# Three sets' scores masked by ScalarE and GpSimd, and two more parts of the first product by seven multiplications

## The chip, the cores and the metric

The kernel runs on one core of a Trainium2 chip. The metric is the device time in microseconds of one execution; the time of a kernel is the median of its runs. Engines are called by their names or by the profile's: PE (TensorE; PEld is its weight load), DVE (VectorE), ACT (ScalarE), POOL (GpSimd), SP (SyncE, which here only issues DMAs).

## The reference

Linear attention with decay for 4 batches, 8 heads, 768 positions and 64 dimensions, in blocks of 64, followed by a feed-forward layer on its output (3072 tokens of 512 features, 2048 hidden):

```
for b in range(nb):
    intra = einsum('bhic,bhjc->bhij', qb, kb) * Dmask      # Dmask: lam ** (i - j) where i >= j, else 0
    intra = einsum('bhij,bhjd->bhid', intra, vb)
    inter = einsum('bhid,bhde->bhie', qb * lam_pow, kv_state)
    out[:, :, sl] = intra + inter
    kv_state = lam_block * kv_state + einsum('bhsd,bhse->bhde', kb * rev_pow, vb)
h = x @ w_in                      # x: out as [3072, 512]
out = (h / (1 + exp(-h))) @ w_out
```

Inputs and output are float32; the kernel multiplies in bfloat16 and sums in float32.

## The kernel before, in words

The 3072 tokens are 24 units of 128 positions (6 position blocks of 4 batches). The attention takes two units at a time, a **set**: sets 0 to 3 hold blocks 0 and 1 of one batch each, sets 4 to 11 hold one block (2 to 5) of two batches. The feed-forward layer takes four units at a time, a **group** of 512 tokens; groups 2 to 5 are position blocks 2 to 5. In each set q, k and v are loaded by SP (L422), cast and scaled by powers of lam (L718 to L739; the powers are arranged so that the mask within a block becomes a plain triangle of ones and zeros), and q and k are turned, from set 6 on by a DMA transpose (L777). Then TensorE computes scores and state updates (`first_part`, L783), the scores are masked into the tile `st` (`after_first`, L869: two instructions on DVE that multiply the PSUM tile by the triangle `tri`), the states are carried on (`yf`, `y`, `xf`, `xe`), and TensorE computes the outputs (`second_part`, L819) into `x_ps`, which is copied as `xt` (L928), the input of the feed-forward layer. From set 7 on, the second part of one set and the first part of the next are one burst on TensorE.

The first product (x times w_in, then silu into the tiles `g`) has two forms. `product1` (L969) is the plain one: per tile of 128 hidden features four matmuls of 512 columns (L989). `product1_spared` (L1073) is the other: it splits the matrices into 2 x 2 blocks and needs seven block products where the plain form needs eight (`product`, L1106: four matmuls of 256 columns each), with sums of blocks of w_in (`wsum`, made once by DVE, L1053) and of xt (`xsum`, four DVE instructions for each group, L1089), and with copies (`keep`, L1118), totals (`h`, L1131) and four silus for each part. A group's first product has four parts. Before the change, parts 0, 1 and 2 of group 4 and all of group 5 are made by seven. The second product (`product2`, L1197, `products_of`, L1241) is made by seven for all units but the first four; its sums on the left side are the tiles `s`, and its results go through `osb` to the output.

No instruction is placed by hand. Every piece of work is a task with a key, engines that may take it with a cost on each, tasks that it depends on, and buffers from pools of fixed size. A planner (L39 to L215) runs through a timetable of its own before anything is issued: on each engine, whenever it is free, it takes the ready task with the smallest key whose buffers are to be had; a task that names several engines goes to the one that would be done first. The order found in this way is the program's order on every engine, and on the chip each engine works through its own queue in that order. Keys are built from a unit's rank (0 to 23) and from constants: LEAD and HURRY (how far ahead of its rank a set from 4 on is prepared, `key_of`, L521), EAGER and CALM (the same for the small work of the second product), ONTO (from which unit on the first sum of the second product stays in PSUM, L1297), HOLD (how many `two` buffers the first four units by seven hold, L1245), SUMS_ON (the key of the wsum). Pools `one` and `sp` limit how many tiles of the plain and the split first product are open at once. The wsum tiles live in the pool `rb`, which also holds the raw loads of q, k and v.

The mask, as it stands before:

```
def mask(e, p):
    tt(e, o.st_of()[:, p].rearrange("p b m i -> p (b m) i"), o.st_ps[p].tile.rearrange("p b m i -> p (b m) i"),
       tri[:, None, :].to_broadcast([128, nb * NP, 64]), AL.mult)

o.masked = [add((s - 0.9, 0), {"DVE": 0.15 + w / 950}, lambda e, p=p: mask(e, p), deps=[t], bufs=[o.st_ps[p], o.st])
            for p in range(2)]
```

Of the kernel before, what the change touches and what calls it, by code (L numbers as in the profile page):

```python
# [11 lines left out]
AL = mybir.AluOpType  # L12
# [26 lines left out]
class Planner:  # L39
# [16 lines left out]
    def add(self, key, on, fn, deps=(), bufs=(), nbytes=0, kind=None, prior=(), late=0.0):  # L56
        key = key if isinstance(key, tuple) else (key,)
        on = on if nbytes else {e: d - self.OVERLAP.get(e, 0.0) for e, d in on.items()}
        t = Task(key, on, fn, deps, list(bufs) + [b.with_ for b in bufs if b.with_], nbytes, kind, prior, late)
        for b in t.bufs:  # L60
            b.left += 1
        self.tasks.append(t)
        return t
# [155 lines left out]
def kernel(  # L219
# [10 lines left out]
    nc = tc.nc  # L230
# [5 lines left out]
    NP = H // 2  # L236
# [7 lines left out]
    PAIRED = 2  # L244
    SETS = [[(0, b), (1, b)] for b in range(B)] + [[(n, b), (n, b + 1)] for n in range(PAIRED, NB) for b in (0, 2)]
    GROUPS = [SETS[0] + SETS[1], SETS[2] + SETS[3]] + [[(n, b) for b in range(B)] for n in range(PAIRED, NB)]
    FRESH, TURNED, ALONE, LEAD = 4, 6, 6, 4.25
    SEQUENCE = "s0 s1 i0a@1.1 i0b i1a i1b i2a i2b i3a i3b o0 o1 s2@1.0 o2 o3 s3 s4"
    POOLS = dict(bank=8, ra=3, rb=6, kq=3, kqT=3, vd=3, st=3, xe=6, xf=3, y=2, yf=2,
                 xt2=2, xt4=2, g=18, s=12, m=3, osb=3, one=3, two=8, att=6, sp=3)  # L250
    BY_POOL, PLAIN = (), 4
    CASTING, SUMS_AFTER, HURRY, SUMS_ON, HOLD, ONTO = 12, 16, 0.0, 9.0, 1, 24
    EARLY, PACE = 1.0, 1.0
    OPEN, FILLED, SCALED = 4, True, (1,)
    QUERIES = (0, 1, 2, 3)
# [1 line left out]
    ON_ACT = ()  # L257
    LAZY, FINE, SAFE, EASY, TAIL, SURE = 2.0, True, 1.3, -0.22, 0.9, 1.5
    XE_2, XE_B, XE_P = {"ACT": 0.42, "DVE": 0.35}, 0.1, False
    MIXED, APART, KEPT = (0, 1, 2), 1, 'yf'  # L260
    EAGER, CALM, ON = 10.0, 1.0, 0.0
    SHARED = ()
    BY_SET = {0: 8, 1: 16}
    WHOLE = ()
    RATED = (3, 4)
    S3_IN = "rb"

    ctx.enter_context(tc.manual_schedule())
    const = ctx.enter_context(tc.tile_pool(name="const", bufs=1))
# [4 lines left out]
    add = plan.add  # L274

    def tile_of(b, shape, dt, name):
# [9 lines left out]
        out=lam_sb[0:1],  # L286
        in_=bass.AP(tensor=lam.tensor, offset=lam.offset, ap=[[0, 1]] + list(lam.ap)),
# [7 lines left out]
    halves = [slice(0, 64), slice(64, 128)]  # L295
# [12 lines left out]
    for t in xe_tiles[4:]:  # L308
# [6 lines left out]
        out=ident, in_=ident, compare_op=AL.not_equal, fill=1.0,  # L315
        base=0, pattern=[[-1, 128]], channel_multiplier=1,
# [6 lines left out]
    for c, r in enumerate(halves):  # L323
        nc.gpsimd.affine_select(
            out=tri[r], in_=tri[r], compare_op=AL.is_ge, fill=0.0,
            base=0, pattern=[[1, 64]], channel_multiplier=-1,
# [5 lines left out]
    for r in halves:  # L332
        nc.gpsimd.iota(iota_2[r], pattern=[[0, 1]], base=0, channel_multiplier=2)
        for a in range(2):
            for b in range(2):
                nc.gpsimd.affine_select(
                    out=tri_2[r, a, b], in_=tri_2[r, a, b], compare_op=AL.is_ge, fill=0.0,
                    base=-1 if a > b else 0, pattern=[[1, 64]], channel_multiplier=-1,
# [27 lines left out]
    def copy(e, o, i):  # L366
        if e == "ACT":
            nc.scalar.activation(o, i, AF.Copy)  # L368
        elif e == "DVE":
            nc.vector.tensor_copy(o, i)  # L370
        else:
            nc.gpsimd.tensor_copy(o, i)

    def tt(e, o, a, b, op):
        (nc.vector if e == "DVE" else nc.gpsimd).tensor_tensor(o, a, b, op=op)  # L375
# [26 lines left out]
    raw = {}  # L402
    sp_last = []
# [53 lines left out]
    for m, x in enumerate(SEQUENCE.split() + [f"s{i}" for i in range(len(sets))]):  # L457
        x, _, behind = x.partition("@")
        j, part = int(x[1:].rstrip("ab")), x[-1] if x[-1] in "ab" else ""
# [11 lines left out]
        elif behind and behind[0] in "io":  # L471

            ts, wt = wload[behind[0], int(behind[1])], w_in_bf if behind[0] == "i" else w_out_bf
            at = wt[0:1, 0, 512 * int(behind[1]):512 * int(behind[1]) + 1] if behind[0] == "i" else wt[0:1, 4 * int(behind[1]), 0:1]
            held = [add((m - 100, -1), {"SP": 2.2}, lambda e, g=gates, at=at: nc.sync.dma_start(
                out=gate_w[0:1, g:g + 1], in_=at), deps=ts, prior=sp_last[-1:])]
            gates += 1
        elif behind:
            u, i = map(int, behind.split("."))
            rs, loads = raw[u]  # L480
            tile = lambda b=rs[i]: b.tile[:, 0, 0, 0:1] if len(b.tile.shape) == 4 else b.tile[:, 0, 0:1]
            if x[0] == "s":
                held = [add((m - 100, -1), {"SP": 2.2}, lambda e, g=gates, tile=tile: nc.sync.dma_start(
                    out=gate[0:1, g:g + 1], in_=tile()[0:1]), deps=loads[i], bufs=[rs[i]], prior=sp_last[-1:])]
# [12 lines left out]
    groups = GROUPS  # L497
# [7 lines left out]
    def after(stage, ts):  # L505
        ts = ts if isinstance(ts, list) else [ts]
        for t in ts:
            t.deps += chain.get(stage, [])
        chain[stage] = ts
# [9 lines left out]
    infos = []  # L519
# [349 lines left out]
    def after_first(o, t):  # L869

        n, bs, nb, s = o.n, o.bs, o.nb, o.s
        w = 512 * nb // 2

        def mask(e, p):
            tt(e, o.st_of()[:, p].rearrange("p b m i -> p (b m) i"), o.st_ps[p].tile.rearrange("p b m i -> p (b m) i"),
               tri[:, None, :].to_broadcast([128, nb * NP, 64]), AL.mult)

        o.masked = [add((s - 0.9, 0), {"DVE": 0.15 + w / 950}, lambda e, p=p: mask(e, p), deps=[t], bufs=[o.st_ps[p], o.st])
                    for p in range(2)]
        after("m", o.masked)  # L880
        bp = bs[0] // 2
        b0 = bs[0] % 2
        xe_in, xf_in, xe_ready, xf_ready = carry[n - 1, bp]
        o.xe = [xe_in, Buf("xe")]
        dcost = 0.15 + w / 950

        def of(b, dt=F32):
            return tile_of(b, [128, nb, NP, 64], dt, b.pool)

        def blocks(b, src, deps, bufs, i):  # L890

            def go(e, r):
                if b.tile is None:
                    b.tile = xe_tiles[b.slot]
                copy(e, b.tile[halves[r], b0:b0 + nb, :, halves[r]], src()[halves[r]])

            return [add((s - 0.9, i), dict({"ACT": 0.2 + w / 1200, "DVE": XE_B + w / 1900}, **({"POOL": 0.25 + w / 1000} if XE_P else {})), lambda e, r=r: go(e, r),
                        deps=deps, bufs=[b] + bufs) for r in range(2)]

        o.xe_done = list(xe_ready)  # L900
        mf = Buf("yf")
        tm = add((s - 0.9, 1), {"DVE": dcost}, lambda e: tt(e, of(mf), o.d_of(0), xf_in.tile, AL.add),
                 deps=[t] + xf_ready, bufs=[o.d_ps[0], mf, xf_in])
        o.xe_done += blocks(o.xe[1], lambda: mf.tile, [tm], [mf], 2)
        if n == NB - 1:
            return

        y = Buf("y")
        ty = add((s - 0.9, 3), {"DVE": dcost}, lambda e: tt(e, of(y), o.d_of(1), mf.tile, AL.add),
                 deps=[t, tm], bufs=[o.d_ps[1], mf, y])  # L910
        xe_n, xf_n, xe_t, xf_t = carry[n, bp] = Buf("xe"), Buf("xf"), [], []
        rate = lam_be[:, None, :, None].to_broadcast([128, nb, NP, 64])

        def xf_of():
            return tile_of(xf_n, [128, 2, NP, 64], F32, "xf")[:, b0:b0 + nb]

        def next_states(e):
            if e == "DVE":
                tt(e, xf_of(), y.tile, rate, AL.mult)
                return  # L920
            for m in range(NP):
                by_rate(e, xf_of()[:, :, m], y.tile[:, :, m], lam_be[:, m:m + 1])

        tf = add((s - 0.9, 4), {"DVE": dcost, **({"ACT": 1.1} if n in RATED else {})}, next_states, deps=[ty], bufs=[y, xf_n])
        xf_t.append(tf)
        xe_t += blocks(xe_n, xf_of, [tf], [xf_n], 5)
# [21 lines left out]
    for si, o in enumerate(infos):  # L948
# [6 lines left out]
        else:  # L955
            if open_ is None:
                after_first(o, burst((o.s - 0.5, 0), [first_part(o)]))
            else:
                a, b = second_part(open_), first_part(o)
                t = burst((o.s - 0.5, 0), [a, b])  # L960
# [90 lines left out]
            W[f"A{i + 1}{j + 1}"] = lambda r=r, c=c: w_in_bf[:, c, r]  # L1051

    def sums_of_w_in():  # L1053
        bufs = {name: Buf(S3_IN if name == "S3" else "rb") for name in ("S1", "S2", "S3", "S4")}
        for name, b in bufs.items():
            W[name] = lambda b=b: tile_of(b, [128, 2, 1024], BF16, "wsum")
        loads = [t for i in range(4) for t in wload["i", i]]
        done = {"A11": loads, "A12": loads, "A22": loads}
        issued, casts = [sp_last[-1]], [t for ts in infos[-1].ck for t in ts]

        def total(name, a, b, op, deps, on):
            done[name] = [add((on, 8), {"DVE": 0.7}, lambda e, ks=ks: tt(
                e, W[name]()[:, ks], W[a]()[:, ks], W[b]()[:, ks], op), deps=deps, prior=issued, bufs=[bufs[name]])
                          for ks in (0, 1)]

        on = SUMS_ON
        total("S1", "A21", "A22", AL.add, loads, on)
        total("S2", "S1", "A11", AL.subtract, done["S1"], on + 0.1)
        total("S3", "A11", "A21", AL.subtract, casts, on + 0.2)
        total("S4", "A12", "S2", AL.subtract, done["S2"], on + 0.3)  # L1070
        return bufs, done
# [242 lines left out]
        m3 = product(6, R, "S4", "B22", False, [e22])  # L1314
        result(0, hi, R, b2, [m3, c2])

    for gi in range(len(groups) - 2):
        product1(gi)
    for t in waits:
        t.deps += gs[0, 0][2]  # L1320
        t.bufs.append(gs[0, 0][0])
        gs[0, 0][0].left += 1
    made = sums_of_w_in()
    left = [j for j in range(4) if j not in MIXED]
    if left:
        product1(len(groups) - 2, [m for j in left for m in (2 * j, 2 * j + 8)])
    if MIXED:
        product1_spared(len(groups) - 2, *made, MIXED)
    product1_spared(len(groups) - 1, *made, range(4))
    by_rank = sorted(rank, key=rank.get)  # L1330
    for u in by_rank[:PLAIN]:
# [49 lines left out]
```

## Time and profile before

| what | value |
|---|---|
| time, median of 3 runs | 201.17 us (201.0 to 202.44) |
| the profiled execution | 200.99 us, its span 199.2 us |
| matmuls of the first product, plain, 512 columns | 176 |
| matmuls of the first product by seven, 256 columns | 196 |
| masks of scores on DVE, 128x512 from PSUM | 32 |
| POOL in the span | 13.7 us busy, nothing after about 35 us |
| granted TensorE clock | 1.00 |

The profile is of one execution. Its page gives, in this order, the busy time of each engine, the span in 40 slices (a digit is tenths of busy time), the DMA queues, the chain of work that ended last, and the costliest groups of instructions: line, engine, operation, output<-input with shapes, count | busy us, mean ns of one | idle time of the engine ahead of them and what ended it. Other views of the same trace are the chain in order of time, the waits (who waited for whom: us in total, times, longest), and the timeline (start, length, engine and instruction). Lines are those of the kernel before.

### The profile page before, as it was taken

To read this page: it belongs to the slowest core of one execution; us is meant where nothing else is said; L and a number is where in the kernel's file an instruction comes from. 1 tells how busy PE (TensorE), PEld (TensorE's weight loads), DVE (VectorE), ACT (ScalarE), POOL (GpSimd) and SP (SyncE) were. 2 spreads that over 40 slices of the span, in tenths; PEclk is the share of its full clock that TensorE was granted. 3 is DMA by queue.
4 is the path that set the end of the run, shared out by engine and by line. 5 is a ranking of instruction groups with operands and counts; after the bars stand their busy time and mean duration, and the time that the engine had idled before them with its cause. 6 is when DMAs were issued, how large, how long until landed. Compare 5 with 4: busy or idle time off the path is not lost.

```text
span 199.2 us, 5953 instructions
## 1 busy us (share of the span) xinstructions
PE 188.4 (95%) x2564; PEld 139.7 (70%) x2564; DVE 146.1 (73%) x302; ACT 127.4 (64%) x241; POOL 13.7 (7%) x36
## 2 busy tenths in 40 slices
PE   0699799999999999999999999999999999999993
PEld 0467565447778785667778648478888688888882
DVE  7799230278997999939998854999948991986611
ACT  2857767218899947648383785536797847866220
POOL 7087003000000000000000000000000000000000
PEclk9999999999999999999999999999999999999999
DMA  5999999999999999999999999901911001003304
GB/s 155 290 241 194 215 216 217 277 215 236 259 262 233 227 238 199 248 162 211 187 207 221 204 261 195 268 4 59 155 56 56 0 3 53 0 5 105 105 30 133
DMA packets 84894, 32.89 MB, mean 165 GB/s; under 512 B 62852, under 2 KB 84356, under 8 KB 84868
## 3 DMA queue, kind: packets, MB, share of 16 engines
q1 hardware_dynamic: 75074, 22.55, 59.1%
q0 software_dynamic: 4288, 4.20, 12.8%
q10 hardware_dynamic: 5506, 5.77, 9.2%
q8 instruction: 20, 0.33, 0.7%
q14 instruction: 6, 0.05, 0.1%
HBM read 27.26 MB, written 6.29 MB: 168 GB/s over the span
## 4 chain that ended last, share of the span: by engine, by line
PE 87%; DVE 4%; DMA 4%; ACT 1%; SPq 1%; issue 1%
PE o_ps L1259 31%; PE h_ps L989 29%; PE h_ps L1112 11%; PE o_ps L1029 7%; DMA raw<-in_q_dram 4%; DVE st L375 2%; PE x_ps L842 2%; PE d_ps L802 1%; PE x_ps L834 1%; SPq L417 1%; PE st_ps L812 1%; PE tr L768 1%; PE tr L566 1%; ACT xe L368 1%; ACT xt L368 1%
## 5 line engine op out<-in xcount | busy, mean ns | idle before, releaser
L989 PE MATMUL h_ps<-xt,w_in_bf 128*128 128x256 bf16 (+1 forms) x368 | 63.2, 324 | 1.1 <-DVE xt L370 0.6
L989 PEld LDWEIGHTS <-w_in_bf 128*128 128x128 bf16 x368 | 35.0, 98 | 22.4 <-issue 1.3
L1259 PEld LDWEIGHTS <-g 128*128 128x128 bf16 x320 | 31.1, 98 | 4.8
L1006 ACT ACTIVATE g<-h_ps 128x512 bf16<-128x512 f32 x44 | 25.3, 595 | 8.5 <-PE h_ps L989 8.4
L1259 PEld LDWEIGHTS <-s 128*128 128x128 bf16 x240 | 23.4, 98 | 3.0
L375 DVE TENSOR_TENSOR st<-st_ps,tri 128x512 bf16<-128x512 f32 x32 | 20.5, 684 | 5.0 <-PE st_ps L812 5.0
L375 DVE TENSOR_TENSOR vd<-raw,lam_v 128x512 bf16<-128x512 f32 x24 | 15.9, 686 | 7.8 <-DMA raw<-in_v_dram 7.8
L1259 PE MATMUL o_ps<-w_out_bf,s 128*128 128x256 bf16 x160 | 19.1, 273 | 0.0
L1259 PE MATMUL o_ps<-wsum,g 128*128 128x256 bf16 x160 | 18.9, 273 | 0.0
L375 DVE TENSOR_TENSOR kq<-raw,lam_q 128x512 bf16<-128x512 f32 x24 | 15.8, 684 | 4.3 <-DMA raw<-in_q_dram 4.0
L1259 PE MATMUL o_ps<-w_out_bf,g 128*128 128x256 bf16 x160 | 18.6, 273 | 0.0
L1004 ACT ACTIVATE g<-h_ps 128x512 bf16<-128x512 f32 x24 | 13.8, 597 | 6.4 <-PE h_ps L989 6.3
L368 ACT ACTIVATE m<-o_ps 128x512 f32<-128x512 f32 (+1 forms) x16 | 8.5, 528 | 14.4 <-PE o_ps L1259 14.3
L375 DVE TENSOR_TENSOR osb<-o_ps,m 128x512 f32<-128x512 f32 (+1 forms) x18 | 10.8, 599 | 9.2 <-ACT m L368 5.2
L368 ACT ACTIVATE xt<-x_ps 128x512 bf16<-128x512 f32 x16 | 9.8, 640 | 9.1 <-DVE osb L375 3.2
L1029 PE MATMUL o_ps<-w_out_bf,g 128*128 128x512 bf16 x64 | 15.5, 380 | 0.0
L375 DVE TENSOR_TENSOR h<-h_ps,m 128x512 f32<-128x512 f32 x14 | 9.6, 688 | 7.3 <-ACT m L368 7.1
L1112 PEld LDWEIGHTS <-wsum 128*128 128x128 bf16 x112 | 10.9, 98 | 1.5
L368 ACT ACTIVATE kqT<-tr 128x512 bf16<-128x512 bf16 x19 | 10.4, 598 | 2.0 <-PE tr L566 1.5
L368 ACT ACTIVATE kq<-raw 128x512 bf16<-128x512 f32 x16 | 9.7, 627 | 2.2 <-DMA raw<-in_k_dram 2.0
L1112 PE MATMUL h_ps<-xsum,wsum 128*128 128x256 bf16 x84 | 11.0, 273 | 0.0
L1138 ACT ACTIVATE g<-h 128x512 bf16<-128x512 f32 x14 | 8.7, 628 | 2.3 <-DVE h L375 2.2
(98 smaller groups left out, 257.5 us busy)
## 6 DMA issues: line engine op xcount, KB each, us to landing
raw<-in_q_dram SPq DMA_DIRECT2D x12, 512.0 KB, 7.7
raw<-in_k_dram SPq DMA_DIRECT2D x12, 512.0 KB, 7.9
raw<-in_v_dram SPq DMA_DIRECT2D x12, 512.0 KB, 7.4
out_dram<-osb ACTq DMA_DIRECT2D x20, 256.0 KB, 4.4
w_in_bf<-in_moe_w_in_dram POOLq DMA_DIRECT2D x8, 256.0 KB, 8.9
w_out_bf<-in_moe_w_out_dram POOLq DMA_DIRECT2D x4, 512.0 KB, 14.2
out_dram<-osb ACTq DMA_DIRECT2D x4, 128.0 KB, 1.7
out_dram<-osb SPq DMA_DIRECT2D x4, 128.0 KB, 2.0
```

Source lines behind the costliest of these rows:

```text
L368: nc.scalar.activation(o, i, AF.Copy)
L375: (nc.vector if e == "DVE" else nc.gpsimd).tensor_tensor(o, a, b, op=op)
L417: nc.sync.dma_start(out=rs[i].tile.rearrange("p h e d -> p h (e d)"), in_=x[i])
L566: nc.tensor.transpose(t[:, m, a], o.kq_of()[:, i, m, a], ident)
L842: nc.tensor.matmul(x_of(c)[:, j, m, :], lhsT=o.xe[c].tile[:, (bs[0] + j) % 2, m, :], rhs=o.kqT_of()[:, 1, j, m, halves[c]], start=False, s ...
L989: nc.tensor.matmul(t[:, j, :], lhsT=w_in_bf[:, ko, 128 * m:128 * m + 128], rhs=xt[gi].tile[:, ko, ts], start=ko == 0 and (j == 0 or len(ko ...
L1004: nc.scalar.activation(t[:, :, ts], bank.tile, AF.Silu)
L1006: nc.scalar.activation(t[:, x, :], bank.tile[:, 0], AF.Silu)
L1029: nc.tensor.matmul(t, lhsT=g.tile[:, j, 128 * gp:128 * gp + 128], rhs=w_out_bf[:, ko, :], start=(ko == 0), stop=(ko == KO - 1))
L1112: nc.tensor.matmul(t[:, j, :], lhsT=W[w]()[:, k2, f:f + 128], rhs=X(r)[:, k2, :], start=first and j == 0 and k2 == 0, stop=True, skip_grou ...
L1138: nc.scalar.activation(o, src(), AF.Silu)
L1259: nc.tensor.matmul(t[:, i_, :], lhsT=src(j)[:, k2, 128 * r:128 * r + 128], rhs=W[w]()[:, 2 * j + k2, :], start=first and i_ == 0 and j == ...
```

## The change

The mask of sets 6, 8 and 10 is taken from DVE: ScalarE copies the scores from PSUM into `st` (two instructions of 128x512), and GpSimd then clears in place, in each half of the partitions, what lies behind the query (two affine_select instructions of 64 partitions by 1024). Group 4's first product is made by seven in all its four parts, and part 0 of group 3 too. The sums of w_in wait for the load of set 9 and no longer for the last load. Several constants that set keys and pools are changed.

```
-    FRESH, TURNED, ALONE, LEAD = 4, 6, 6, 4.25
+    FRESH, TURNED, ALONE, LEAD = 4, 6, 6, 3.5
-                 xt2=2, xt4=2, g=18, s=12, m=3, osb=3, one=3, two=8, att=6, sp=3)
+                 xt2=2, xt4=2, g=18, s=12, m=3, osb=3, one=4, two=8, att=6, sp=2)
-    CASTING, SUMS_AFTER, HURRY, SUMS_ON, HOLD, ONTO = 12, 16, 0.0, 9.0, 1, 24
+    CASTING, SUMS_AFTER, HURRY, SUMS_ON, HOLD, ONTO = 12, 16, 1.0, 6.0, 0, 20
-    MIXED, APART, KEPT = (0, 1, 2), 1, 'yf'
-    EAGER, CALM, ON = 10.0, 1.0, 0.0
+    MIXED, APART, KEPT = (0, 1, 2, 3), 1, 'yf'
+    EAGER, CALM, ON = 12.0, 2.0, 0.0
+    SUMS_IN, BEHIND = 'rb', 9
+    THIRD = (0,)
+    CUT, CUT_TIME = (6, 8, 10), 1.1
...
-        o.masked = [add((s - 0.9, 0), {"DVE": 0.15 + w / 950}, lambda e, p=p: mask(e, p), deps=[t], bufs=[o.st_ps[p], o.st])
-                    for p in range(2)]
+        if o.si in CUT:
+
+            def taken(e, p):
+                copy(e, o.st_of()[:, p].rearrange("p b m i -> p (b m) i"), o.st_ps[p].tile.rearrange("p b m i -> p (b m) i"))
+
+            def cut(e, r):
+                x = o.st_of()[r].rearrange("p h b m i -> p (h b m) i")
+                nc.gpsimd.affine_select(out=x, in_=x, compare_op=AL.is_ge, fill=0.0, base=0,
+                                        pattern=[[0, 2 * nb * NP], [1, 64]], channel_multiplier=-1)
+
+            tk = [add((s - 0.9, 0), {"ACT": 0.17 + w / 1200}, lambda e, p=p: taken(e, p), deps=[t], bufs=[o.st_ps[p], o.st])
+                  for p in range(2)]
+            o.masked = [add((s - 0.9, 0), {"POOL": CUT_TIME}, lambda e, r=r: cut(e, r), deps=tk, bufs=[o.st]) for r in halves]
+        else:
+            o.masked = [add((s - 0.9, 0), {"DVE": 0.15 + w / 950}, lambda e, p=p: mask(e, p), deps=[t], bufs=[o.st_ps[p], o.st])
+                        for p in range(2)]
...
-        issued, casts = [sp_last[-1]], [t for ts in infos[-1].ck for t in ts]
+        issued, casts = raw[BEHIND][1][2][-1:], [t for ts in infos[BEHIND].ck for t in ts]
...
-    for gi in range(len(groups) - 2):
+    for gi in range(len(groups) - 3):
         product1(gi)
...
+    for gi, parts in ((3, THIRD), (4, MIXED)):
+        left = [j for j in range(4) if j not in parts]
+        if left:
+            product1(gi, [m for j in left for m in (2 * j, 2 * j + 8)])
+        if parts:
+            product1_spared(gi, *made, parts)
     product1_spared(len(groups) - 1, *made, range(4))
```

More of the change, by code (lines that the diff above doesn't have):

```diff
@@ L1053, in sums_of_w_in @@
     def sums_of_w_in():
-        bufs = {name: Buf(S3_IN if name == "S3" else "rb") for name in ("S1", "S2", "S3", "S4")}
+        bufs = {name: Buf(SUMS_IN) for name in ("S1", "S2", "S3", "S4")}
         for name, b in bufs.items():
@@ L1323 @@
     made = sums_of_w_in()
[L1324 to L1328, printed above, removed]
+    for gi, parts in ((3, THIRD), (4, MIXED)):
[4 more added lines that the diff above has]
+            product1_spared(gi, *made, parts)
     product1_spared(len(groups) - 1, *made, range(4))
```

## The prediction

> **What bounds the kernel now.** Read first: busy shares and the chain that ended last, then the chain in order of time, the groups by form, the waits after 76 us, and a piece of the timeline.
>
> ```profile
> PE 188.4 (95%) x2564; PEld 139.7 (70%) x2564; DVE 146.1 (73%) x302; ACT 127.4 (64%) x241; POOL 13.7 (7%) x36
> ...
> PE   0699799999999999999999999999999999999993
> ...
> PEclk9999999999999999999999999999999999999999
> ...
> PE 87%; DVE 4%; DMA 4%; ACT 1%; SPq 1%; issue 1%
> ```
>
> TensorE is busy 95% of the span at full clock and carries 87% of the chain. What is not TensorE lies in the first 22 us and the last three.
>
> ```profile
> 76.58 6.20 PE h_ps L989 x28
> ...
> 98.15 3.45 PE h_ps L989 x16
> ...
> 143.55 4.37 PE h_ps L1112 x40
> ...
> 183.91 12.24 PE o_ps L1259 x112
> 196.16 0.02 issue
> 196.18 0.42 DVE osb L375
> ```
>
> The chain in order of time (start, us, what): from 22.4 to 196.16 us it is TensorE almost without a break. It gives issue intervals: 3.45/16 = 215.6 ns for a matmul of 512 columns, 4.37/40 = 109.3 ns for 256 (12.24/112 says the same). The mean durations below (379 and 273) overlap and cannot be added.
>
> ```profile
> L989 PE MATMUL h_ps<-xt,w_in_bf 128*128 128x512 bf16 x176 | 40.3, 379 | 0.2 <-ACT xe L368 0.2
> ...
> L1006 ACT ACTIVATE g<-h_ps 128x512 bf16<-128x512 f32 x44 | 25.3, 595 | 8.5 <-PE h_ps L989 8.4
> ...
> L375 DVE TENSOR_TENSOR st<-st_ps,tri 128x512 bf16<-128x512 f32 x32 | 20.5, 684 | 5.0 <-PE st_ps L812 5.0
> ...
> L336 POOL TENSOR_SCALAR_AFFINE_SELECT tri<-tri 64x64 f32<-64x64 f32 x8 | 1.6, 241 | 0.1
> ...
> L314 POOL TENSOR_SCALAR_AFFINE_SELECT ident<-ident 128x128 bf16<-128x128 bf16 x1 | 0.3, 287 | 0.1
> ```
>
> ```profile
> PEld L989 <- DVE xt L370: 0.4, 1, 0.4
> ...
> PE h_ps L989 <- ACT xe L368: 0.2, 1, 0.2
> ```
>
> Waits between 76 and 185 us: beyond "issue" the list has only these for TensorE.
>
> ```profile
> 75.38 1.04 PE L989 MATMUL h_ps<-xt,w_in_bf 128*128 128x256 bf16 x8
> ...
> 75.82 0.69 DVE L370 CAST xt<-x_ps 128x512 bf16<-128x512 f32 x1
> ...
> 76.57 3.63 PE L989 MATMUL h_ps<-xt,w_in_bf 128*128 128x512 bf16 x16 [0.15 <-ACT xe L368]
> ```
>
> The one place where TensorE stands: eight matmuls from 75.38 are issued by 75.38 + 8 x 0.109 = 76.25, and block 2's first product starts at 76.57, when set 5's copy of xt (75.82 + 0.69) is done: 0.32 us. So the bound is TensorE's own issue, and no edit to another engine can give more than this.
>
> **The change part by part.** The profiled execution took 200.99 us (span 199.2, 1.79 around it); the median is 201.17. I sum against 200.99. The rest goes by the order in which the changed program's instructions stand on each engine. Up to 73.6 us TensorE's order is the same, and so are the counts of fillers, of second-product matmuls (560 + 64) and of everything else on TensorE but this:
>
> 1. *Two more parts in seven* (block 4's last, block 3's first). 32 matmuls of 512 go, 56 of 256 come: 56 x 0.1093 - 32 x 0.2156 = 6.12 - 6.90 = **-0.78 us**, all on the path.
>
> 2. *The stall at 76.25.* In the new order set 5's second part stands after four matmuls of the split product in place of eight, and twelve follow it in place of eight: 12 x 0.109 = 1.31 us of cover for the copies of xt, where 0.87 was 0.32 short; VectorE's queue before that copy is unchanged in length (a 0.69 osb for a 0.69 kq, a 0.42 s for the other). **-0.32 us**; the bound above is nothing.
>
> 3. *Scores of sets 6, 8, 10.* VectorE loses 6 masks of 684 ns. ScalarE gains 6 copies of 128x512 from PSUM, 0.60 each (row L1006). GpSimd gains 6 clears of 64 partitions x 1024. No row has this shape. A line through the two affine_select rows, 241 ns at 64 elements and 287 at 128, is 0.72 ns per element on a base of 0.195: 0.93 us. Bounds: 0.29 (no growth at all) to 16 x 0.241 = 3.9 (all growth). I take 0.93, since the two rows differ by 46 ns for twice the elements. Path from scores to use: 0.2 + 2 copies (0.60 + 0.50) + 2 clears (1.9) + waits 0.3 = 3.5 us. Cover, summed from the issue intervals in the new order: set 6 from 91.7 to 98.1 = 6.4 us; set 8 from 110.8 to 125.2; set 10 from 132.5 to 155.9. Nothing on the path; it would be for set 6 above (6.4 - 1.6)/2 = 2.4 us a clear.
>
> 4. *What the two parts cost beside TensorE.* Four xsum for block 3 (0.42), four h (0.69) on VectorE, some six copies m (0.60) on ScalarE. Counted over the whole order, VectorE comes to 145 us (4.1 less for masks, 1.7 and 2.8 more, the rest small), ScalarE to 127.4 + 8.1 = 135.5, 68% of the span. In the densest stretch (two parts of block 4 at once, 32 matmuls, 3.5 us) ScalarE must give two silus and two copies between products: at 0.53 apart the last copy is done 3.0 us in, and the product that overwrites its bank starts at 3.06. It holds, with nothing to spare: +0.1.
>
> 5. *Sums of w_in made behind set 9's load.* Eight wsum (0.69) move on VectorE from 138-152 us to about 105-119, and take four of the six raw buffers while sets 10 and 11 are still to load. I find those loads issued in time (transposes of set 10 at about 121, first used at 131.6). The last wsum stands just ahead of the h that the seventh product of block 3's part waits for: VectorE's queue from set 8's yf (111.0) to that h adds up to 7.7 us, h ends at 119.5, the product is due at 120.1: slack 0.1 to 0.5. I put +0.2 there.
>
> 6. *LEAD, HURRY, EAGER, CALM, HOLD, pools one and sp.* They change order alone. On SP the transposes of sets 6 and 7 now stand back to back (about 82 and 86, 3.6 us each by the earlier rows) ahead of the load of set 8's queries, which goes out near 89.8 where it went at 79.75. Loads behind a transpose landed 5.4 and 8.2 us after issue (113.6 to 119.0, 100.4 to 108.6): 95.2 to 98.0. VectorE reaches that query at about 96.2, and queued behind it are the sums that the third product of the next four units needs at 104.6, with some 0.5 us to spare. So 0 to 1.3; I take +0.2. Earlier, the first four units' third product moves from 82.6 to 80.7, and its last sum ends at 80.5: +0.1.
>
> 7. *ONTO 20.* In the last four units the first product's sum is copied into the second's bank. That product now waits for a copy (0.42 on VectorE), but 0.87 us of another product lies between. The end (last matmul, osb 0.42, store) is the same: 0.
>
> Sum: -0.78 - 0.32 + 0.1 + 0.2 + 0.2 + 0.1 = -0.5, so 200.99 - 0.5 = **200.5**. New stalls together are bounded by 0 and about 1.3 + 0.5 + 0.3 without the rivals below.
>
> **The rivals.**
>
> *GpSimd's clears hold VectorE off (slower).* While a clear runs, VectorE's instructions with two operands in SBUF (s, xsum, xf, vd, kq) would stand until it ends. Nothing in this trace shows it either way, as GpSimd computes nothing after 5 us but two one-element copies. Price: up to 0.93 a clear, 1.9 a set. Set 8's clears (about 115 to 117) fall among the vd, xf and wsum that precede the h of point 5: 0.9 (half of them caught) to 1.8 on the path. Set 6's (93 to 95) fall on s and xf before the sums of point 6: 0.4 to 1.3. Set 10's: VectorE is some 2 us ahead, 0. Together 1.3 to 3.1 on 200.5: 201.8 to 203.6, middle **202.6**. It makes the kernel slower than before from 0.5 us of such loss on. The Trainium skill has this as a rule: "SBUF — State Buffer", section "Who interferes with whom", says that a VectorE instruction with two SBUF inputs contends with a GpSimd instruction that reads SBUF, and that whichever comes second is blocked in full until the first is done. By that rule the sum would be this rival's; by the rows alone, 200.5. Against it stands that many of VectorE's neighbours there (yf, y, h, osb) read PSUM, and that ops that come late can be absorbed by slack I counted too low.
>
> *Set 8's load late.* If it lands 8.2 us or more after issue and the transposes take 5.2 (rows at 95 and 108) and not 3.6, VectorE stands 1.8 to 3 us, 1.3 to 2.5 of it on the path: 201.0 to 202.8, middle **201.9**. For it: SP's queue. Against it: fewer loads are in flight then.
>
> *The clear is priced by elements.* At 3.9 us a clear, set 6 is late by 2 x (3.9 - 2.4) = 3.0, and the rest as above: **204**.
>
> *The time falls by more than 1%.* TensorE's order leaves no room: 200.99 - 0.78 - 0.32 = 199.9 with no new stall.
>
> **How the numbers follow.** Forecast 0.58 (own range 199.8 to 201.3), clears hold VectorE 0.22, late load 0.12, dear clear 0.06, beyond the floor 0.02. Range 199.8 to 202.9: it leaves out the last two, and about half of what the clears' case has above 202.6. About 1% is what a measurement of this kernel can tell from no change: 199.2 and 203.2. Faster: 0.02. Slower: the dear clear and a quarter of the clears' case, 0.11. Same: 0.87.
>
> **What would show it.** In the groups, 252 matmuls of the split product and 144 of 512 columns at the same intervals; last matmul near 195.7. No wait at 76. Clears of 0.9 to 1.0 us; VectorE's sums beside them at 0.42 (forecast) or at 1 us and more (rival). Waits of TensorE on "DVE s" near 104.6 or on "DVE h" near 120 add up to about half a microsecond, not two. I am wrong if the interval of the matmuls changes, if the first 73 us differ, or if TensorE stands anywhere for more than 1 us.

## The result: slower by half a per cent, and the profile after

| | before | changed |
|---|---|---|
| time, median (16 runs each) | 201.03 us (200.88 to 202.44) | 202.18 us (201.87 to 203.6) |
| the profiled execution | 200.99 us | 202.0 us |
| its span | 199.2 us | 200.3 us |

The ratio is 1.0051, interval 1.0031 to 1.0071. The forecast was 0.5 us less; it became about 1 us more. The page after, in the order of the page before, with the group of the new clears:

```profile
PE 187.5 (94%) x2588; PEld 141.9 (71%) x2588; DVE 149.9 (75%) x302; ACT 133.4 (67%) x255; POOL 21.1 (11%) x42
...
PE   0689799999999999999989997999999999999993
...
PEclk9999999999999999999999999999999999999999
...
L888 POOL TENSOR_SCALAR_AFFINE_SELECT st<-st 64x1024 bf16<-64x1024 bf16 x6 | 7.4, 1229 | 97.6 <-ACT st L371 97.4
```

TensorE's busy time fell by 0.9 us. DVE's came to 149.9 where the prediction counted 145. TensorE's row has a new 8 (about 100 us) and a new 7 (about 120); a third digit, near 10 us, lies ahead of all that changed on TensorE. The clears take 1.23 us, not 0.93. The groups by form say that the planned work itself came as forecast: 144 matmuls of 512 columns, and six masks fewer on DVE at the old length.

```profile
L1006 PE MATMUL h_ps<-xt,w_in_bf 128*128 128x512 bf16 x144 | 33.9, 379 | 0.6 <-DVE osb L378 0.6
...
L378 DVE TENSOR_TENSOR st<-st_ps,tri 128x512 bf16<-128x512 f32 x26 | 16.4, 686 | 1.4 <-PE st_ps L815 1.4
```

In the chain in order of time, the work that ended last was all TensorE from 22.4 us on; now it leaves TensorE for DVE:

```profile
117.60 1.62 DVE xf L378
...
120.36 1.29 DVE wsum L378 x2
121.65 0.61 DVE h L378
122.26 0.04 issue
122.30 0.60 PE h_ps L1129 x4
...
185.83 11.37 PE o_ps L1276 x104
197.19 0.02 issue
```

The last matmul ends at 197.19 (before 196.16, +1.03). The waits from 73 to 190 us name what TensorE waited for (engine, line, releaser: us, times, longest):

```profile
PE h_ps L1129 <- DVE h L378: 1.2, 1, 1.2
...
PE h_ps L1006 <- DVE osb L378: 0.6, 1, 0.6
```

Counted from the issue of the matmuls, with the prediction's intervals, the two stands (stretches in which TensorE issues nothing) are longer: the matmuls before them are issued by 100.35 and 120.96, the next begin at 101.15 and 122.30, so 0.80 and 1.34, together 2.14 us. The timeline around them (start, length, engine, instruction, idle time before it) shows why; first what happens beside set 6's clears:

```profile
75.05 5.84 PE L1006 MATMUL h_ps<-xt,w_in_bf 128*128 128x256 bf16 x32
...
93.43 2.42 POOL L888 TENSOR_SCALAR_AFFINE_SELECT st<-st 64x1024 bf16<-64x1024 bf16 x2 [58.42 <-ACT st L371]
...
93.35 0.69 DVE L378 TENSOR_TENSOR y<-d_ps,yf 128x512 f32<-128x512 f32 x1
93.96 0.88 DVE L378 TENSOR_TENSOR s<-g 128x512 bf16<-128x512 bf16 x1
94.76 1.62 DVE L378 TENSOR_TENSOR xf<-y,lam_be 128x512 f32<-128x512 f32 x1
96.31 0.41 DVE L378 TENSOR_TENSOR s<-s,g 128x512 bf16<-128x512 bf16 x1
...
100.41 0.69 DVE L378 TENSOR_TENSOR osb<-o_ps,m 128x512 f32<-128x512 f32 x1
...
101.15 1.02 PE L1006 MATMUL h_ps<-xt,w_in_bf 128*128 128x512 bf16 x4 [0.64 <-DVE osb L378]
```

The first line is the stall of before at 76.25: gone, 32 matmuls run through. From 93.43 to 95.85 GpSimd clears. In that time y, which reads one operand from PSUM, takes its usual 0.69. But s takes 0.88 and xf 1.62, where the s after the clears takes 0.41, and an xf of this shape 0.68 in the first experiment below: 0.46 + 0.94 = 1.4 us lost in DVE's queue. Some four us later TensorE waits for osb, the last in that queue. The same at set 8, and at set 10 without harm:

```profile
115.94 2.75 POOL L888 TENSOR_SCALAR_AFFINE_SELECT st<-st 64x1024 bf16<-64x1024 bf16 x2 [20.09 <-ACT st L371]
116.78 0.90 DVE L378 TENSOR_TENSOR vd<-raw,lam_v 128x512 bf16<-128x512 f32 x1
117.60 1.62 DVE L378 TENSOR_TENSOR xf<-y,lam_be 128x512 f32<-128x512 f32 x1
...
121.57 0.68 DVE L378 TENSOR_TENSOR h<-h_ps,m 128x512 f32<-128x512 f32 x1
...
137.77 1.25 DVE L378 TENSOR_TENSOR xsum<-xsum,xt 128x512 bf16<-128x512 bf16 x1
138.94 1.35 DVE L378 TENSOR_TENSOR xsum<-xt 128x512 bf16<-128x512 bf16 x1
```

vd (0.68 there) and xf lose 0.22 + 0.94 = 1.16 us, and the h that ends this queue comes 1.34 too late. The difference is what VectorE still carried from set 6: its y starts 41.12 us after the 32 matmuls of 75.05 (116.17), without clears 40.10 after them (115.76 from 75.66), so it is 1.02 late where TensorE is 0.80 late. The two xsum (0.42 without company) lose 1.8, and no matmul waits.

### The profile page after: what moved, and what is told of

It reads as the page before. It is cut to its first block, busy times and chain, and to the rows that moved or that the text cites. A ratio compares the mean times of both kernels' runs of the same rounds, so it can differ in the third digit from the quotient of the medians.

```text
span 200.3 us, 6033 instructions
## 1 busy us (share of the span) xinstructions
PE 187.5 (94%) x2588; PEld 141.9 (71%) x2588; DVE 149.9 (75%) x302; ACT 133.4 (67%) x255; POOL 21.1 (11%) x42
## 5 line engine op out<-in xcount | busy, mean ns | idle before, releaser
L1006 PE MATMUL h_ps<-xt,w_in_bf 128*128 128x256 bf16 (+1 forms) x336 | 56.6, 318 | 1.6 <-DVE osb L378 0.6
L1006 PEld LDWEIGHTS <-w_in_bf 128*128 128x128 bf16 x336 | 31.9, 98 | 18.7 <-issue 2.2
L1023 ACT ACTIVATE g<-h_ps 128x512 bf16<-128x512 f32 x36 | 20.8, 594 | 5.7 <-PE h_ps L1006 5.5
L378 DVE TENSOR_TENSOR h<-h_ps,m 128x512 f32<-128x512 f32 x18 | 12.4, 691 | 10.0 <-PE h_ps L1129 5.2
L888 POOL TENSOR_SCALAR_AFFINE_SELECT st<-st 64x1024 bf16<-64x1024 bf16 x6 | 7.4, 1229 | 97.6 <-ACT st L371 97.4
L378 DVE TENSOR_TENSOR st<-st_ps,tri 128x512 bf16<-128x512 f32 x26 | 16.4, 686 | 1.4 <-PE st_ps L815 1.4
L1021 ACT ACTIVATE g<-h_ps 128x512 bf16<-128x512 f32 x24 | 13.7, 596 | 5.4 <-PE h_ps L1006 5.3
L1129 PEld LDWEIGHTS <-wsum 128*128 128x128 bf16 x144 | 14.1, 98 | 3.2 <-issue 1.1
L1129 PE MATMUL h_ps<-xsum,wsum 128*128 128x256 bf16 x108 | 13.4, 273 | 0.0
L1155 ACT ACTIVATE g<-h 128x512 bf16<-128x512 f32 x18 | 11.2, 625 | 2.6 <-DVE h L378 2.3
L378 DVE TENSOR_TENSOR s<-g 128x512 bf16<-128x512 bf16 x20 | 8.7, 445 | 4.5 <-ACT g L1023 3.3
```

What stands on the lines that cost most here:

```text
L888: nc.gpsimd.affine_select(out=x, in_=x, compare_op=AL.is_ge, fill=0.0, base=0, pattern=[[0, 2 * nb * NP], [1, 64]], channel_multiplier=-1)
L1006: nc.tensor.matmul(t[:, j, :], lhsT=w_in_bf[:, ko, 128 * m:128 * m + 128], rhs=xt[gi].tile[:, ko, ts], start=ko == 0 and (j == 0 or len(ko ...
L1021: nc.scalar.activation(t[:, :, ts], bank.tile, AF.Silu)
L1023: nc.scalar.activation(t[:, x, :], bank.tile[:, 0], AF.Silu)
L1129: nc.tensor.matmul(t[:, j, :], lhsT=W[w]()[:, k2, f:f + 128], rhs=X(r)[:, k2, :], start=first and j == 0 and k2 == 0, stop=True, skip_grou ...
L1155: nc.scalar.activation(o, src(), AF.Silu)
```

## The experiments

Theory L: the clears hold VectorE's instructions with two operands in SBUF, and their lateness is the 2.14 us. Rival O: the new order itself is too tight (the sums, the loads, the split parts), and the clears only stand beside it.

**The clears left out.** The scores of sets 6, 8 and 10 stay unmasked; the order on all other engines stays that of the changed kernel.

```
-                nc.gpsimd.affine_select(out=x, in_=x, compare_op=AL.is_ge, fill=0.0, ...)
+                pass
```

> The changed kernel without its six clears on GpSimd (the scores of sets 6, 8 and 10 stay unmasked); every other engine's queue is the same, instruction for instruction. Theory L (the clears hold VectorE's instructions with two SBUF operands, and TensorE waits for what stands behind them): xf falls from 1.62 to 0.69 us at both places, TensorE's waits at 100.4 (0.80 us) and 121.0 (1.34 us) go but for some 0.2 us at the second, the last matmul ends near 195.3 in place of 197.19, time 200.0 to 200.4. Theory O (VectorE's queue is simply too long there in the new order, whatever GpSimd does): the two waits stay above 0.5 us each, time 201.6 to 202.2.

Measured: 199.84 us, ratio 0.9932 (0.991 to 0.9954). Its timeline:

```profile
94.57 0.42 DVE L378 TENSOR_TENSOR s<-g 128x512 bf16<-128x512 bf16 x1
94.90 0.68 DVE L378 TENSOR_TENSOR xf<-y,lam_be 128x512 f32<-128x512 f32 x1
...
120.00 0.68 DVE L378 TENSOR_TENSOR h<-h_ps,m 128x512 f32<-128x512 f32 x1
...
120.78 0.60 PE L1129 MATMUL h_ps<-xt,wsum 128*128 128x256 bf16 x4
```

Both instructions are back at their own length, TensorE waits for nobody after 73 us, and h (done at 120.68) is 0.1 us ahead of its matmul. From the 32 matmuls at 75.05 (here 75.66) to the last matmul the changed kernel takes 122.14 us and this one 120.01: 2.13 less, the two stands. VectorE is busy for 145.8 us in place of 149.9: 4.1 less, against 1.4 + 1.16 + 1.8 that the three sets were read to lose. Rival O falls: the order without clears beats the kernel before.

**The same clears, without reading.** GpSimd writes zeros over the tiles.

```
-                nc.gpsimd.affine_select(out=x, in_=x, compare_op=AL.is_ge, fill=0.0, ...)
+                nc.gpsimd.memset(x, 0.0)
```

> The six clears replaced by six GpSimd memsets of the same tile region, which write SBUF and read nothing (the scores of sets 6, 8 and 10 become zero); all other queues the same. Theory L in its narrow form (VectorE's second operand and GpSimd's read share one way): VectorE's instructions keep their length, time 200.0 to 200.5. Theory L in a wide form (any GpSimd access to SBUF holds them): xf above 1 us again, time 201.2 to 202.2. Theory O: 201.6 to 202.2.

Measured: 200.64 us, ratio 0.9957 (0.9925 to 0.9989), lowest run 199.78; one of the twelve took 326.63, and why is not known. The median is a little above the range that was expected.

```profile
94.75 1.94 POOL L888 MEMSET st<- 64x1024 bf16 x2 [59.88 <-ACT st L371]
95.29 0.41 DVE L378 TENSOR_TENSOR s<-g 128x512 bf16<-128x512 bf16 x1
95.62 0.68 DVE L378 TENSOR_TENSOR xf<-y,lam_be 128x512 f32<-128x512 f32 x1
```

s and xf lie wholly inside GpSimd's 1.94 us and lose nothing; TensorE waits for nobody here either. From the 32 matmuls (here at 76.38) to the last (196.39) it takes 120.01 us, exactly as without clears: nearly all that this profiled execution (201.2) is longer than that one (200.44) lies before them. So for these products it is neither that GpSimd is busy nor that it writes. What affine_select does beyond memset is to read the tile; no other GpSimd instruction that reads was tried.

A cast within SBUF is another matter. Beside set 10's memsets two of them take 1.38 us, where they take 0.75 in the changed kernel (140.56, behind its clears):

```profile
136.79 1.95 POOL L888 MEMSET st<- 64x1024 bf16 x2 [18.39 <-ACT st L371]
...
137.97 1.38 DVE L373 CAST kq<-raw 128x512 bf16<-128x512 f32 x2
```

The first of the two starts during the second memset and is the one held, for 0.63 us; the xsum just before it keep their 0.42. So a GpSimd instruction that only writes can hold a cast, though it held no product here. No matmul waits for it.

**Each clear twice.** The second of each two changes nothing in the result.

```
-                nc.gpsimd.affine_select(out=x, in_=x, ...
+                for _ in range(2): nc.gpsimd.affine_select(out=x, in_=x, ...
```

> Each clear issued twice (the second changes nothing), so GpSimd is busy some 4.9 us a set; all other queues the same. Theory L: twice as many of VectorE's instructions are held, 1.2 to 1.8 us more at each set, so TensorE's waits at 100 and 121 grow by about as much each and one near 139 appears: 204 to 206. Theory O: as the changed kernel, 202 to 202.4 (the masked scores of set 6 come 6.4 us after the scores, just as long as their cover).

Measured: 209.46 us, ratio 1.0398 (1.0347 to 1.0449): the direction of L, but more than it gave. The two waits grew; the one expected near 139 did not come.

```profile
93.55 5.23 POOL L888 TENSOR_SCALAR_AFFINE_SELECT st<-st 64x1024 bf16<-64x1024 bf16 x4 [58.57 <-ACT st L371]
...
94.88 1.62 DVE L378 TENSOR_TENSOR xf<-y,lam_be 128x512 f32<-128x512 f32 x1
96.42 1.35 DVE L378 TENSOR_TENSOR s<-s,g 128x512 bf16<-128x512 bf16 x1
97.69 1.35 DVE L378 TENSOR_TENSOR g<-g 128x512 bf16<-128x512 bf16 x1
...
121.13 1.36 DVE L373 CAST kq<-raw 128x512 bf16<-128x512 f32 x1
```

Each further clear costs one further instruction about 0.93 us. A cast from one SBUF tile to another (0.41 without company) is held as well. TensorE's two stands are 2.35 and 3.24 us by the matmuls' issue, 5.6 together. From the 32 matmuls near 75 to the last matmul this kernel takes 127.55 us, 7.5 more than the one without clears. The other 1.9 lie mostly behind the second stand, as stretches of the same execution show (start:end, length, busy time of PE, PEld, DVE, ACT, POOL, then the granted clock):

```profile
123.00:126.00 3.00, 0.11 (x2) 0.10 (x1) 2.96 (x5) 0.00 (x0) 0.49 (x1) 1.00 0.08 12
126.00:129.00 3.00, 2.81 (x9) 1.28 (x9) 1.94 (x4) 1.66 (x4) 0.00 (x0) 0.52 0.11 21
129.00:132.00 3.00, 3.00 (x19) 1.77 (x18) 1.84 (x5) 2.25 (x4) 0.00 (x0) 0.91 1.01 190
```

Behind the stand of 3.24 us the granted clock is 0.52 for 3 us and 0.91 for the next 3: 0.48 x 3 + 0.09 x 3 = 1.7 us. Behind this kernel's stand of 2.35 us (from 103.10 to 109.10) and behind the changed kernel's of 0.80 and 1.34 us it is 1.00. The profiled execution took 208.0; what the median has beyond it was not traced.

**The mask as before, the rest as changed.** 

```
-    CUT, CUT_TIME = (6, 8, 10), 1.1
+    CUT, CUT_TIME = (), 1.1
```

> The changed kernel with no set cut (masks of all sets on VectorE again), ordered anew by the planner; the two more parts in seven and all constants stay. Theory L: the two more parts keep their 0.78 us and the stall at 76 stays away, VectorE has 3.6 us more to do in all: 200.1 to 200.9. Theory O: VectorE, longer still by the masks, keeps TensorE waiting: 201.8 to 203.

Measured: 201.89 us, ratio 1.0038 (1.0014 to 1.0062): by the numbers, what O gave, and outside what L gave. But the planner made another order out of it, and its chain (of an execution of 203.53 us) runs elsewhere:

```profile
177.85 1.32 PE h_ps L1129 x12
...
179.20 1.12 ACT g L1155 x2
180.32 0.50 ACT h_ps L371
...
180.85 3.65 PE h_ps L1129 x32
```

The chain leaves TensorE for ScalarE near 180, and TensorE waits for it there (0.38 us in the waits) and at 126 (0.78), places where the changed kernel has no wait. So this run does not tell the theories apart; it says that without the cut these constants give an order that is no better. Only runs that keep the other queues as they are (the three before this one) speak clearly about the clears.

**The clears with the order of before.** The constants and parts of before, with CUT (6, 8, 10).

> The kernel before with the cut alone (sets 6, 8 and 10 copied by ScalarE and cleared by GpSimd), its constants and its parts in seven as before; the planner orders anew. Theory L (clears hold VectorE): 1.2 to 1.8 us of VectorE's time lost at each set where two-operand work stands beside the clears, part of it on the path: 201.3 to 203. Theory O (only the queue's length counts): VectorE has 3.6 us less to do, 200.4 to 201.2.

Measured: 202.26 us, ratio 1.0058 (1.0029 to 1.0086), inside what L gave. Set 6's clears meet other neighbours here, and do the same to them; set 8's meet an xf:

```profile
89.96 2.68 POOL L888 TENSOR_SCALAR_AFFINE_SELECT st<-st 64x1024 bf16<-64x1024 bf16 x2 [54.95 <-ACT st L371]
90.27 1.37 DVE L373 CAST kq<-raw 128x512 bf16<-128x512 f32 x1
91.56 1.34 DVE L378 TENSOR_TENSOR s<-g 128x512 bf16<-128x512 bf16 x1
...
113.33 2.77 POOL L888 TENSOR_SCALAR_AFFINE_SELECT st<-st 64x1024 bf16<-64x1024 bf16 x2 [20.69 <-ACT st L371]
...
114.42 0.68 DVE L378 TENSOR_TENSOR xf<-y,lam_be 128x512 f32<-128x512 f32 x1
```

TensorE then waits 0.48 us at 93.56 and 0.57 at 107.96, for DVE; the last matmul is 1.3 later than before. The second wait lies 15 us behind set 6's clears; VectorE's queue has no gap of note between, so it can be the rest of the same loss, but no run of this order without clears shows it. The xf at set 8 keeps its 0.68: it starts at 114.42, the second clear at 114.54, and here it is the clear that takes longer, 1.57 us where most take 1.14 to 1.21. Here the one that started first kept its length.

**The two parts in seven and the earlier sums alone.** CUT empty, the old constants of keys and pools.

> The kernel before with the two more parts in seven alone (and the sums of w_in behind set 9's load, without which they have no weights), masks on VectorE, its old constants; ordered anew. If the 0.78 us of TensorE's time is all that counts: 200.0 to 200.6. If the work that the two parts bring to ScalarE and VectorE costs waits, as in the run with no cut: 201 to 202.5.

Measured: 200.81 us, ratio 1.0007 (0.9985 to 1.003): no change, and between the two ranges that were expected. Of the 0.78 us saved 0.17 reaches the last matmul (195.99): in this order TensorE waits 0.3 us for a wsum near 106 and 0.25 for m at 112.66. The part that saves is real only in an order that has room for it.

**VectorE in GpSimd's place.** ScalarE still copies the scores, but VectorE multiplies the bf16 tile by a bf16 triangle, where GpSimd's clears stood in the order.

```
+    tri_bf = const.tile([128, 64], BF16, name="tri_bf")
+    nc.gpsimd.tensor_copy(tri_bf, tri)
...
-                nc.gpsimd.affine_select(out=x, in_=x, compare_op=AL.is_ge, fill=0.0, ...)
+                tt("DVE", x, x, tri_bf[:, None, :].to_broadcast([128, nb * NP, 64]), AL.mult)
```

> The changed kernel's order kept, with each clear on GpSimd replaced, at its place in the order, by a VectorE product of 128x512 in bf16 of the copied scores with the triangle (two a set, some 0.35 us each in the queue): nothing runs on GpSimd. Theory L: VectorE loses 0.7 us a set where the clears cost it 1.4, 1.2 and 1.8; TensorE's waits become 0.1 to 0.3 at 100 and 0.7 to 1.0 at 121 (0.80 and 1.34 before): 200.7 to 201.3. Theory O: as the changed kernel, 201.6 to 202.2.

Measured: 200.85 us, ratio 0.9988 (0.9966 to 1.001), as expected: the product takes 0.42 in bf16 from SBUF where the mask from PSUM took 0.68, and nothing is held. In the profiled execution (204.24 us) the wait that was at 121 is 0.7 us, as expected, and the one at 100 is not listed. The same with the planner told of it (a DVE task of 0.43):

> The same as the run before it, but the planner knows that these products are VectorE's (0.43 each) and orders anew. A new order may have waits of its own (0 to 1.5 us); with none the time is 200.0: 200.0 to 201.5 under both theories. It tells whether some order with the two parts in seven and no clears on GpSimd beats the kernel before.

Measured: 204.37 us, ratio 1.0159 (1.0135 to 1.0184): outside the 200.0 to 201.5 that were expected. In the new order TensorE waits for ScalarE and DVE in seven places after 73 us, 0.25 to 0.69 us each and 2.7 together; which choice of the planner brings them was not looked into. Then the fixed order again, with one thing moved: set 8's two products stand behind the critical h.

```
+            if o.si == 8:
+                later.extend(o.masked)
...
+                if gi == 3:
+                    for t in later:
+                        t.prior.append(e22)
```

> The run with the products in bf16 on VectorE, with set 8's two products moved behind the h that TensorE waits for at 121 (they stand after it in VectorE's queue, and set 8's masked scores are first read near 125); TensorE's and ScalarE's queues the same. Theory L with the slack as measured without clears: the wait at 121 goes but for 0.2, that at 100 stays 0 to 0.3: 199.9 to 200.4, faster than both kernels. If the masks are then too late for set 8's second part, a wait of up to 1 us at 125: 200.8 to 201.2.

Measured: 200.79 us, ratio 0.9978 (0.9946 to 1.0009), lowest 200.15: the median is above the 199.9 to 200.4 of theory L, and the runs spread over more than the expected gain. In the profile the wait at 121 is gone: the waits list none of TensorE after 73 us. Last, set 10's clears given back to GpSimd, where the held instructions have 2 us to spare:

> The same, with set 10's clears on GpSimd again, where VectorE was some 2 us ahead of its readers. Theory L: VectorE's xsum beside them take 1.2 to 1.4 us in place of 0.42, and TensorE does not wait for it: the same time as the run before within 0.2, 199.9 to 200.5. If a held VectorE costs time wherever it is: 201 to 201.7.

Measured: 200.52 us, ratio 0.9968 (0.9942 to 0.9994).

```profile
136.26 2.62 POOL L893 TENSOR_SCALAR_AFFINE_SELECT st<-st 64x1024 bf16<-64x1024 bf16 x2 [102.16 <-DVE osb L380]
...
136.51 1.36 DVE L380 TENSOR_TENSOR xsum<-xt 128x512 bf16<-128x512 bf16 x1
137.80 1.35 DVE L380 TENSOR_TENSOR xsum<-xt,xsum 128x512 bf16<-128x512 bf16 x1
```

Held as ever, 0.94 and 0.93 us, and the waits list none of TensorE after 73 us. From the 32 matmuls to the last one it takes 120.44 us (75.19 to 195.63), the run before it 120.43: the held xsum cost nothing there. Without any clears it was 120.01; what is left are stands of under 0.2 us. This version is faster than both kernels, by 0.3% on the kernel before, with an interval that comes near to no change.

## Why the prediction went wrong

The step that failed is point 3's "Nothing on the path". The path from the scores to their use was indeed covered (no wait of TensorE on st after the change); VectorE's other work, which the point did not put on the path, was held by the clears and cost TensorE 2.14 us. By its own sign, that TensorE stands nowhere for more than 1 us, the prediction was wrong: it stood 1.34. The stated range, 199.8 to 202.9, holds the measured 202.18 only because it took in part of the rival's case; the forecast's own ended at 201.3. The choice that went with it was to give the rival "GpSimd's clears hold VectorE off" 0.22 and the forecast 0.58. The two reasons set against the rival do not hold: neighbours that read PSUM do keep their length (y here, osb with the order of before), but xf, vd and s stand between them in the same queue; and the slack hoped for took up some 0.6 of set 6's 1.4 us, but at h it is 0.1 by the kernel without clears, the low end of the 0.1 to 0.5 of point 5.

- Point 1 (-0.78) and point 2 (-0.32): right. From the matmuls at 73.56 (74.28) to the last, the kernel before takes 122.60 us and the one without clears 121.39: -1.21 where the two terms give -1.10. With the clears' 2.13 that makes 0.92 more than before, and 0.11 of the last matmul's 1.03 lies ahead of 73.6 us (the matmuls of 73.56 start at 73.67 after the change).
- Point 3: a clear took 1.23, inside the bounds 0.29 to 3.9, and its size was not the matter. The hold put 2.14 us on the path where the sum has nothing.
- Point 4 (+0.1): TensorE has no wait on ScalarE beyond 73 us; 0. Its 145 us for VectorE was right too: 145.8 without clears; the 149.9 are the hold.
- Point 5 (+0.2): without clears 0; with them 1.34, at the very place named.
- Point 6 (+0.2 and +0.1): set 8's query was not late; VectorE reaches its kq at 97.86 without a wait. The tight spot behind it was not the sums at 104.6 but the osb at 100.41, whose bank a first product needs at 100.35. From 1.4 us of loss 0.80 remained there. Near 80.7, where 0.1 was put, TensorE has no wait.
- Point 7 (0): right; from the last matmul to the end nothing changed.
- The rival's own sum: set 6 0.4 to 1.3 (0.80), set 8 0.9 to 1.8 (1.34), set 10 nothing (nothing): 202.6 forecast for it, 202.18 measured. "It makes the kernel slower than before from 0.5 us of such loss on" underrates the order's room: without clears it is 1.2 us better, so that the loss had to pass this.

The Trainium skill's rule ("SBUF — State Buffer", section "Who interferes with whom") that a VectorE instruction with two SBUF inputs contends with a GpSimd instruction that reads SBUF, and not with one that only writes it, agrees with both halves of these runs: xf 1.62 beside affine_select, 0.68 beside memset. The same section of the Trainium skill counts copies and casts among those that can contend; the cast at 1.36 in place of 0.41 beside affine_select agrees, and so does the one held by a memset.

What stays open: which of the changed constants makes the order's room, since none was tried by itself; what slows the replanned order of the bf16 mask; and whether other GpSimd instructions that read SBUF hold VectorE as affine_select does.

## What to carry to other kernels

Before work goes to an idle GpSimd, list what VectorE does in that window: beside affine_select, products with two operands in SBUF and casts within SBUF lost here up to 0.94 us for each clear of 1.23 us; beside memset the products lost nothing, but a cast lost 0.63; those with an operand in PSUM lost nothing. Such a hold costs only what VectorE lacks in slack before the next matmul that waits for it: the same two clears cost nothing at set 10, 0.80 us at set 6, and 1.34 at set 8, of which some 0.2 had been carried over. To judge one suspect in a planned kernel, change it with all other queues held; a replanned order brings waits of its own.

## What the runs showed of the hardware

- affine_select over 64 partitions by 1024 in bf16 took 1.23 us in the mean, a pair of them 2.41 to 2.75, two memsets of that tile 1.94. The prediction's line through two small rows gave 0.93 for one.
- The hold seems to go both ways: a clear that started just behind an xf took 1.57 us, and the xf kept its 0.68.
- A memset, which only writes, left products with two SBUF operands at 0.41 and 0.68 us, and held a cast within SBUF for 0.63 us.
- Between two clears that follow each other VectorE gets one instruction through: a run of them costs it about 0.93 us each (1.35 for 0.42), not the whole of the clears' time.
- A product with a triangle took 0.42 us on a bf16 tile in SBUF, 0.68 on the same shape from PSUM.
- A stand of 3.24 us was followed by a granted clock of 0.52 over 3 us; stands of up to 2.35 were not.
